# Decode attention on one core: K of a head, then V, softmax and PV in the same loop round, V as one 8 MB load

## The chip, the cores and the metric

One core of a Trainium2 chip. The metric is the device time of one execution in microseconds (us). A core has a tensor engine (PE), a vector engine (DVE), a scalar engine (ACT), a general engine (POOL), a sync engine (SP), which here only issues loads, and 16 DMA engines. The kernel before takes 422.17 us (median of 3 runs, 422.05 to 422.44).

## The reference

```python
h = layernorm(x) * (1 + ca) + sa            # x: 2 x 1 x 1024; sa, ca, ... = silu(c) @ w_mod
q = h @ wq                                  # 2 x 32 heads x 128
k, v = k_cache, v_cache                     # 2 x 4 kv heads x 32768 x 128, bf16; 8 q heads share one
p = softmax(q @ k.T * 128 ** -0.5)
x = x + ga * ((p @ v) @ wo)
h = layernorm(x) * (1 + cb) + sb
x = x + gb * (gelu(layernorm(h) @ w1 + b1) @ w2 + b2)
```

There is one new token and a cache of 134 MB. With the weights 178 MB are read; the arithmetic on them is small. "A head" below means one of the 8 pairs of batch and kv head: 8.4 MB of K and 8.4 MB of V.

## The kernel before

A load puts tokens on the 128 partitions. PE transposes K in groups of 8 tiles of 128x128 into PSUM (`tr`), DVE or ACT copies the group to SBUF, and PE multiplies it by the 8 query vectors (`qk`). When all 32 groups of a head are through, the softmax needs the maximum of each query (three small steps over DVE and PE), 8 exps on ACT, and then PE multiplies the probabilities by V (`pv`).

The kernel before hides the softmax: a loop round does K of head i together with softmax and PV of head i-1 ("lagged").

```python
for i in range(NBG):                         # 8 heads; folded into a hardware loop on PE and DVE
    lagged(softmax_1)                        # lagged(): of head i - 1, skipped in the first round
    for cc in range(NCH):                    # 4 chunks of K
        for g8 in range(TPC // 8):           # 8 groups of 8 tiles
            tr(i, cc, g8)
            ...
            if len(pipe) > PIPE: qk(*pipe.pop(0))
            if (cc, g8) == (0, 1):   lagged(softmax_2)
            elif (cc, g8) == (0, 4): lagged(softmax_3)
            elif i and (0, 4) < (cc, g8) and exps: exp(i - 1, exps.pop(0))
        if cc == 1:   lagged(lambda: pv(i - 1, 0), row_sums, lambda: pv(i - 1, 1))
        elif cc == 3: lagged(lambda: pv(i - 1, 2), lambda: pv(i - 1, 3))
    lagged(extract)
    while pipe: qk(*pipe.pop(0))
    lagged(lambda: extract_2(i - 1))
# after the loop: softmax, exps, PV of the last head, then wo, w1, w2
```

Loads are halves of a head (4 MB, 32 KB on each partition), each kind and half with its own 32 KB slot of a ring. SP issues them in program order, each when its slot is free:

```python
SLOT = {("K", 0): 0, ("V", 0): 1, ("K", 1): 2, ("V", 1): 3}
def add_kv(kind, i, hf):
    ...
    add((kind, i, hf), [2, TPC * D], cache[b, g][r0:r0 + 2 * CH_ROWS, :].rearrange("(p c t) d -> p c (t d)", c=2, p=128),
        SLOT[kind, hf] * 32 * KB, f"{kind}{hf}")
# order in the steady state: K half 0 of i, V half 0 of i-1, K half 1 of i, V half 1 of i-1
```

## Time and profile before

| | before |
|---|---|
| median time | 422.17 us |
| span in the profile | 420.3 us |
| DMA, mean over the span | 425 GB/s |
| PE busy | 296.6 us (71%) |
| chain that ended last | 70% DMA |

The page's row of slices cuts the span into 40 pieces. A digit is the busy share in tenths (9 is 90% or more), PEclk is PE's granted clock in tenths of full speed.

```profile
PE   1547429869988767695969686976859693645566
...
PEclk9999999988999997988888896989887888655575
DMA  8999999999999999999999999999999999999995
GB/s 335 430 430 420 437 440 443 411 437 446 409 443 443 424 430 443 433 421 443 440 418 443 437 418 440 443 415 440 449 412 440 446 416 437 423 429 423 428 426 244
```

The DMA row has no hole from the second slice to the last but one. The table of stretches for two heads in the middle says the same, with busy times (the number of instructions in brackets), PE's clock, DMA share and rate:

```profile
core 0: us, PE busy (x) PEld busy (x) DVE busy (x) ACT busy (x) POOL busy (x), PEclk, DMA share, GB/s
179.30:218.00 38.70, 30.43 (x585) 26.71 (x585) 19.18 (x36) 18.36 (x32) 0.31 (x2) 0.86 1.00 433
218.00:256.70 38.70, 30.80 (x584) 27.06 (x584) 19.23 (x36) 18.36 (x32) 0.31 (x2) 0.85 1.00 433
```

No compute engine is full. The groups of instructions (busy us and mean ns of one, then the idle time of the engine just before them and what ended most of it) show who waits:

```profile
L543 PE MATMUL psKT<-ident,K 128*128 128x128 bf16 x2048 | 174.0, 237 | 46.1 <-DMA K<-in_A_k_cache_dram 45.1
...
L576 ACT ACTIVATE E_sb<-S_sb,negm 128x256 bf16<-128x256 f32 x64 | 32.3, 504 | 8.1 <-DVE negm L572 7.1
L586 PE MATMUL psO<-V,E_sb 128*32 128x512 bf16 x512 | 33.9, 401 | 1.3 <-ACT E_sb L576 1.3
```

PE stood for 45 us waiting for K to land. The last head is not lagged, so its timeline (start, duration, engine, line; the idle time before and its releaser in brackets) shows beforehand what a serial round looks like:

```profile
353.67 0.17 DVE L572 TENSOR_SCALAR negm<-psM 128x8 f32<-128x8 f32 x1 [0.48 <-PE psM L571]
353.93 0.51 ACT L576 ACTIVATE E_sb<-S_sb,negm 128x256 bf16<-128x256 f32 x1 [3.60 <-DVE negm L572]
...
358.99 0.23 DVE L593 COPY rsum<-rowsum 128x128 f32<-128x128 f32 x1 [5.16 <-ACT E_sb L576]
359.27 0.59 PE L594 MATMUL psM<-onesf,rsum 128*128 128x1 f32 x2 [5.65 <-DVE rsum L593]
359.79 5.83 PE L586 MATMUL psO<-V,E_sb 128*32 128x512 bf16 x64
```

PE is idle 5.65 us while ACT does 8 exps, and PV's 64 matmuls then take 5.83 us. In the loop 16 of them take 1.05 us at full clock, 4.2 us for 64.

The chain of work that ended last, by engine and by line:

```profile
DMA 70%; PE 26%; ACT 2%; SPq 1%; issue 0%; DVE 0%
DMA K<-in_A_k_cache_dram 51%; PE psKT L543 18%; DMA wo<-in_A_wo_dram 8%; DMA w<-in_B_w_dram 7%; PE psS L555 5%; DMA wmod<-in_w_mod_dram 4%; ACT E_sb L576 1%; PE psO L586 1%; SPq L415 1%; ACT KT_sb L547 1%; PE psO L759 1%; PE psS L680 0%; ACT L576 0%; PE psM L566 0%; ACT S_sb L559 0%
```

### The profile page before, as it was taken

The numbers are of one execution on the slowest core, as the hardware profiler recorded it, in microseconds if no ns is written. First come the engines' busy times: TensorE is split into PE (matmuls) and PEld (weight loads), VectorE is DVE, ScalarE is ACT, GpSimd is POOL, SyncE is SP. The second block draws the span as 40 slices with busy tenths as digits, with TensorE's granted clock in tenths as the row PEclk, the third lists the DMA queues.
The fourth block names the chain that finished last, engine by engine and source line by source line (L and its number), as shares of the span: only waits on it lengthen the run. The fifth ranks groups of instructions, "written<-read, shape, count | busy, mean of one in ns | idle before, by whom it ended". The sixth has DMA issues, their size and how long they took to land.

```text
span 420.3 us, 11591 instructions
## 1 busy us (share of the span) xinstructions
PE 296.6 (71%) x5171; PEld 237.6 (57%) x5171; DVE 166.9 (40%) x347; ACT 156.2 (37%) x269; POOL 6.0 (1%) x31
## 2 busy tenths in 40 slices
PE   1547429869988767695969686976859693645566
PEld 1105109859878657494949575764849492212244
DVE  1102005645676454354536452653555363101311
ACT  2000005538548334551636282446426364200020
POOL 3000000000000000000000000000000000000000
PEclk9999999988999997988888896989887888655575
DMA  8999999999999999999999999999999999999995
GB/s 335 430 430 420 437 440 443 411 437 446 409 443 443 424 430 443 433 421 443 440 418 443 437 418 440 443 415 440 449 412 440 446 416 437 423 429 423 428 426 244
DMA packets 9727, 178.46 MB, mean 425 GB/s; under 512 B 1002, under 2 KB 1009, under 8 KB 2291
## 3 DMA queue, kind: packets, MB, share of 16 engines
q1 hardware_dynamic: 9714, 178.28, 98.9%
q8 instruction: 9, 0.15, 0.1%
q14 instruction: 4, 0.02, 0.0%
HBM read 178.28 MB, written 0.00 MB: 424 GB/s over the span
## 4 chain that ended last, share of the span: by engine, by line
DMA 70%; PE 26%; ACT 2%; SPq 1%; issue 0%; DVE 0%
DMA K<-in_A_k_cache_dram 51%; PE psKT L543 18%; DMA wo<-in_A_wo_dram 8%; DMA w<-in_B_w_dram 7%; PE psS L555 5%; DMA wmod<-in_w_mod_dram 4%; ACT E_sb L576 1%; PE psO L586 1%; SPq L415 1%; ACT KT_sb L547 1%; PE psO L759 1%; PE psS L680 0%; ACT L576 0%; PE psM L566 0%; ACT S_sb L559 0%
## 5 line engine op out<-in xcount | busy, mean ns | idle before, releaser
L543 PE MATMUL psKT<-ident,K 128*128 128x128 bf16 x2048 | 174.0, 237 | 46.1 <-DMA K<-in_A_k_cache_dram 45.1
L543 PEld LDWEIGHTS psKT<-ident,K 128*128 128x128 bf16 x2048 | 133.7, 106 | 53.7 <-DMA K<-in_A_k_cache_dram 49.2
L549 DVE COPY KT_sb<-psKT 128x1024 bf16<-128x1024 bf16 x160 | 107.8, 689 | 107.0 <-PE psKT L543 107.0
L547 ACT ACTIVATE KT_sb<-psKT 128x1024 bf16<-128x1024 bf16 x96 | 98.0, 1021 | 128.4 <-PE psKT L543 128.4
L555 PE MATMUL psS<-qcur,KT_sb 128*128 128x8 bf16 x2048 | 88.1, 167 | 7.7 <-ACT KT_sb L547 6.4
L555 PEld LDWEIGHTS psS<-qcur,KT_sb 128*128 128x128 bf16 x2048 | 79.0, 98 | 12.7 <-ACT KT_sb L547 7.6
L576 ACT ACTIVATE E_sb<-S_sb,negm 128x256 bf16<-128x256 f32 x64 | 32.3, 504 | 8.1 <-DVE negm L572 7.1
L586 PE MATMUL psO<-V,E_sb 128*32 128x512 bf16 x512 | 33.9, 401 | 1.3 <-ACT E_sb L576 1.3
L560 DVE TENSOR_REDUCE m1c<-psS 128x8 f32<-128x512 f32 x32 | 22.1, 690 | 14.8 <-ACT S_sb L559 14.1
L559 ACT ACTIVATE S_sb<-psS 128x512 f32<-128x512 f32 x32 | 18.9, 592 | 18.9 <-PE psS L555 18.9
L586 PEld LDWEIGHTS psO<-V,E_sb 128*32 128x32 bf16 x512 | 12.2, 100 | 13.1 <-issue 4.2
L491 PE MATMUL psS<-wmod,inT 128*32 128x512 bf16 x64 | 8.4, 622 | 11.9 <-DMA wmod<-in_w_mod_dram 11.9
L680 PE MATMUL psS<-wo,atT 128*32 128x512 bf16 x64 | 7.6, 627 | 10.8 <-DMA wo<-in_A_wo_dram 10.8
L462 ACT ACTIVATE stat<-stat 128x2 f32<-128x2 f32 x3 | 0.6, 203 | 35.4 <-DVE stat L461 35.4
L512 PE MATMUL psS<-wq,inT 128*32 128x512 bf16 x64 | 7.6, 627 | 7.1 <-DMA wq<-in_A_wq_dram 6.1
L576 ACT ACTIVATION_READ_ACCUMULATOR E_sb<-S_sb,negm 128x1 f32 x64 | 12.1, 189 | 0.0
L491 PEld LDWEIGHTS psS<-wmod,inT 128*32 128x32 bf16 x64 | 1.3, 112 | 17.9 <-DMA wmod<-in_w_mod_dram 17.4
L680 PEld LDWEIGHTS psS<-wo,atT 128*32 128x32 bf16 x64 | 1.9, 128 | 15.4 <-DMA wo<-in_A_wo_dram 9.4
L606 PE MATMUL psM<-msum,hmat 128*128 128x128 f32 x16 | 4.2, 346 | 7.1 <-DVE msum L601 7.1
L497 ACT ACTIVATE S_sb<-psS 128x512 f32<-128x512 f32 x1 | 0.6, 597 | 22.8 <-DVE S_sb L499 22.8
L499 DVE COPY S_sb<-psS 128x512 f32<-128x512 f32 x1 | 0.7, 692 | 20.6 <-PE psS L491 20.6
L599 DVE TENSOR_SCALAR msum<-psO,mk 128x128 f32<-128x128 f32 x8 | 2.8, 351 | 15.0 <-PE psO L586 15.0
(116 smaller groups left out, 136.4 us busy)
## 6 DMA issues: line engine op xcount, KB each, us to landing
K<-in_A_k_cache_dram SPq DMA_DIRECT2D x16, 4096.0 KB, 25.6
V<-in_A_v_cache_dram SPq DMA_DIRECT2D x16, 4096.0 KB, 32.5
wmod<-in_w_mod_dram SPq DMA_DIRECT2D x8, 1536.0 KB, 16.4
wq<-in_A_wq_dram SPq DMA_DIRECT2D x4, 2048.0 KB, 37.7
wo<-in_A_wo_dram SPq DMA_DIRECT2D x4, 2048.0 KB, 25.3
w<-in_B_w_dram SPq DMA_DIRECT2D x4, 1792.0 KB, 35.8
w<-in_B_w_dram SPq DMA_DIRECT2D x3, 2048.0 KB, 30.4
w<-in_B_w_dram SPq DMA_DIRECT2D x1, 768.0 KB, 27.9
```

The lines of the kernel that those rows point to most:

```text
L415: T.dma("sp", lambda e, dst=dst, src=cur.src: e.dma_start(dst, src), key=cur.sem, writes=[cur.reg], frees=old)
L491: pe(lambda e, w=it.view, k=k, ch=ch, n=n, q=q: e.matmul(bank[n][32 * q:32 * q + 32, :], lhsT=inT[:, k, :], rhs=w[:, ch * 512:(ch + 1) * 512],
L512: pe(lambda e, w=it.view, k=k, ch=ch, n=n, q=q: e.matmul(bank[n][32 * q:32 * q + 32, :], lhsT=inT[:, k, :], rhs=w[:, k % 2, ch * 512:(ch + ...
L543: pe(lambda e, kq=kq, jj=jj, w=kt, t=t: e.transpose(psKT[kq][:, jj * 128:(jj + 1) * 128], w[:, t, :], ident[:, :]), reads=[it.reg, "ident" ...
L547: act(lambda e, src=src: e.activation(KT_sb[g8][:, :, :], src, ACT.Copy), reads=[f"psKT{kq}"], writes=[f"KT_sb{g8}"], sem=f"ev{cc}_{g8}")
L549: dve(lambda e, src=src: e.tensor_copy(KT_sb[g8][:, :, :], src), reads=[f"psKT{kq}"], writes=[f"KT_sb{g8}"], sem=f"ev{cc}_{g8}")
L555: pe(lambda e, t=t, jj=jj: e.matmul(ps[:, t * HPG:(t + 1) * HPG], lhsT=KT_sb[g8][:, jj, :], rhs=qcur[:, :], start=True, stop=True), reads= ...
L559: act(lambda e: e.activation(Sc, ps[:, :].rearrange("p (t h) -> p h t", h=HPG), ACT.Copy), reads=[preg], writes=[f"S_sb{i % 2}_{cc}"], sem ...
L560: dve(lambda e: e.tensor_reduce(m1c[:, :, cc], ps[:, :].rearrange("p (t h) -> p h t", h=HPG), AX.X, ALU.max), reads=[preg], writes=[f"m1c{ ...
L576: act(lambda e: e.activation(E_sb[:, :, h, :], S_sb[j][:, h, :].rearrange("p (u t) -> p u t", t=4), ACT.Exp, bias=negm[:, h:h + 1], scale= ...
L586: pe(lambda e, t4=t4, tg=tg, q=q: e.matmul(psO[32 * q:32 * q + 32, :], lhsT=E_sb[:, tg // 4, :, :].rearrange("p h t -> p (h t)"), rhs=vt[: ...
L680: pe(lambda e, w=it.view, g=g, j=j, hf=hf, q=q: e.matmul(psS[0][32 * q:32 * q + 32, :], lhsT=atT[g][:, j, :], rhs=w[:, j, hf * 512:(hf + 1 ...
```

## The change

Its intent is a simpler loop: K of a head, then its softmax, then its V, all in one round; no second score buffer, no lag. V is wanted only at the end of a round, so it can be one load of 8 MB with 64 KB in a row for each partition, one slot, half as many packets. K stays in two loads. To make a partition's rows of V contiguous, the tokens are dealt to the partitions in another order, for K and V alike.

```diff
-    SLOT = {("K", 0): 0, ("V", 0): 1, ("K", 1): 2, ("V", 1): 3}
-    def add_kv(kind, i, hf):
-        ...
-        add((kind, i, hf), [2, TPC * D], cache[b, g][r0:r0 + 2 * CH_ROWS, :].rearrange("(p c t) d -> p c (t d)", c=2, p=128),
-            SLOT[kind, hf] * 32 * KB, f"{kind}{hf}")
+    def add_k(i, hf):
+        add(("K", i, hf), [2, TPC * D], A_k_cache[i % 2, i // 2].rearrange("(p h c t) d -> h p c (t d)", h=2, c=2, p=128)[hf], hf * 32 * KB, f"K{hf}")
+    def add_v(i):
+        add(("V", i), [NCH, TPC * D], A_v_cache[i % 2, i // 2].rearrange("(p c t) d -> p c (t d)", c=NCH, p=128), 64 * KB, "V")
...
+    for i in range(NBG):
+        add_k(i, 0)
+        add_k(i, 1)
+        add_v(i)
...
     for i in range(NBG):
-        lagged(softmax_1)
         for cc in range(NCH):
             for g8 in range(TPC // 8):
                 tr(i, cc, g8)
                 ...
-                if (cc, g8) == (0, 1): lagged(softmax_2)
-                ...
-            if cc == 1: lagged(lambda: pv(i - 1, 0), row_sums, lambda: pv(i - 1, 1))
-            elif cc == 3: lagged(lambda: pv(i - 1, 2), lambda: pv(i - 1, 3))
-        lagged(extract)
         while pipe:
             qk(*pipe.pop(0))
-        lagged(lambda: extract_2(i - 1))
+        softmax_1()
+        softmax_2()
+        softmax_3()
+        for h in range(HPG):
+            exp(h)
+        row_sums()
+        for cc in range(NCH):
+            pv(i, cc)
+        extract()
+        extract_2(i)
```

(The rest of the diff takes the machinery of the lag out of the helper that places waits, and the last head's copy out of the tail. The order of the loads becomes K, K, V of each head, and the slots of the w1 loads after the loop are dealt anew.)

More of the change, by code (lines that the diff above doesn't have):

```diff
@@ L34 @@
 RING = 160 * 1024
+AHEAD = ("sc2", "sc3", "pk", "ac")
 EVAC_PATTERN = ("dve", "act", "dve", "act", "dve", "dve", "act", "dve")
@@ L41 @@
     LOOPED = ("pe", "dve")
-    PE_KEYS = ("pe", "pl")
     def __init__(self, nc):
@@ L55, in __init__ @@
         self.segments = None
-        self.lag = False
     def key(self, name, given=0, step=None):
@@ L116, in _dep_tokens @@
         if E == "pe":
-            tokens = [t for t in tokens if t[0] not in self.PE_KEYS]
+            tokens = [t for t in tokens if t[0] != "pe"]
         return tokens
@@ L130, in _put @@
         if self.segments is not None and E in self.LOOPED:
-            self.segments[E][-1][1].append(op)
+            self.segments[E].append(op)
         else:
@@ L168, in raw @@
         self._put(E, ("raw", [], fn, None))
-    def part(self, lag):
-        self.lag = lag
-        for E in self.LOOPED:
-            self.segments[E].append((lag, []))
     def fold(self, rounds):
@@ L180, in _fold @@
         first = min(rounds)
-        full = rounds[max(rounds)]
         body = []
-        for n, (lag, ops) in enumerate(full):
-            merged = []
-            for k, (kind, _, fn, extra) in enumerate(ops):
-                offs = {}
-                for it, segs in rounds.items():
-                    same, other = segs[n]
-                    assert same == lag
-                    if not other and lag and it == first:
-                        continue
-                    assert len(other) == len(ops) and other[k][0] == kind and other[k][3] == extra
-                    for key, val in other[k][1]:
-                        off = val - self.step[key] * it
-                        assert offs.setdefault(key, off) == off, (E, n, k, key, it, val, offs)
-                waits = []
-                for key, off in offs.items():
-                    assert self.step[key] * (first + lag) + off > 0, (E, n, k, key, off)
-                    waits.append((key, self.step[key], off))
-                merged.append((kind, waits, fn, extra))
-            if merged:
-                body.append((lag, merged))
+        for k, (kind, _, fn, extra) in enumerate(rounds[max(rounds)]):
+            offs = {}
+            for it, ops in rounds.items():
+                assert len(ops) == len(rounds[first]) and ops[k][0] == kind and ops[k][3] == extra
+                for key, val in ops[k][1]:
+                    off = val - self.step[key] * it
+                    assert offs.setdefault(key, off) == off, (E, k, key, it, val, offs)
+            for key, off in offs.items():
+                assert self.step[key] * first + off > 0, (E, k, key, off)
+            body.append((kind, [(key, self.step[key], off) for key, off in offs.items()], fn, extra))
         self.ops[E].append(("loop", [], body, (first, max(rounds) + 1)))
@@ L218, in _loop @@
     def _loop(self, eng, E, body, bounds):
-        pairs = [w[1:] for _, ops in body for op in ops for w in op[1]]
+        pairs = [w[1:] for op in body for w in op[1]]
         often = [p for p in dict.fromkeys(pairs) if p != (1, 0) and pairs.count(p) > 1]
@@ L227, in wait @@
                 eng.wait_ge(self.sem[w[0]], val[w[1:]] if w[1:] in val else it * w[1] + w[2])
-            for lag, ops in body:
-                def run():
-                    for op in ops:
-                        self._emit(eng, E, op, wait)
-                if lag:
-                    with eng.If(it > bounds[0]):
-                        run()
-                else:
-                    run()
+            for op in body:
+                self._emit(eng, E, op, wait)
     def emit(self, block):
@@ L272, in bass_adaLN_cond__gqa_block_cached__mixer_channel_mlp__decode_kernel @@
     T = Tracker(nc)
-    for name, step, given in (("pe", 64, 0), ("pl", 8, 8), ("dve", 4, 0), ("dl", 4, 4)):
-        T.key(name, given)
-        T.step[name] = step
+    T.step["pe"], T.step["dve"] = 72, 8
     def sb(name, shape, dtype=FP32):
@@ L331, in bass_adaLN_cond__gqa_block_cached__mixer_channel_mlp__decode_kernel @@
     rinv = sb("rinv", [128, 1])
-    S_sb = [sb(f"S_sb{i}", [128, HPG, NT]) for i in range(2)]
-    row = S_sb[0].rearrange("p h n -> p (h n)")
-    ROW = [f"S_sb0_{cc}" for cc in range(NCH)]
+    S_sb = sb("S_sb", [128, HPG, NT])
+    row = S_sb.rearrange("p h n -> p (h n)")
+    ROW = [f"S_sb_{cc}" for cc in range(NCH)]
     E_sb = sb("E_sb", [128, NT // 4, HPG, 4], BF16)
@@ L368, in add @@
         by_key[key] = it
-    SLOT = {("K", 0): 0, ("V", 0): 1, ("K", 1): 2, ("V", 1): 3}
-    def add_kv(kind, i, hf):
-        cache = A_k_cache if kind == "K" else A_v_cache
-        b, g = i % 2, i // 2
-        r0 = hf * 2 * CH_ROWS
-        add((kind, i, hf), [2, TPC * D], cache[b, g][r0:r0 + 2 * CH_ROWS, :].rearrange("(p c t) d -> p c (t d)", c=2, p=128),
-            SLOT[kind, hf] * 32 * KB, f"{kind}{hf}")
+    def add_k(i, hf):
+        add(("K", i, hf), [2, TPC * D], A_k_cache[i % 2, i // 2].rearrange("(p h c t) d -> h p c (t d)", h=2, c=2, p=128)[hf], hf * 32 * KB, f"K{hf}")
+    def add_v(i):
+        add(("V", i), [NCH, TPC * D], A_v_cache[i % 2, i // 2].rearrange("(p c t) d -> p c (t d)", c=NCH, p=128), 64 * KB, "V")
     wm_v = w_mod.rearrange("(p k) n -> p k n", k=KT8)
@@ L383, in bass_adaLN_cond__gqa_block_cached__mixer_channel_mlp__decode_kernel @@
         add(("wq", k), [2, HQ * D], A_wq[k * 256:(k + 1) * 256, :].rearrange("(k p) n -> p k n", p=128), (96 + 16 * k) * KB)
-    add_kv("K", 0, 0)
-    add_kv("K", 0, 1)
-    order = [("K", 0), ("V", 0), ("K", 1), ("V", 1)]
-    early = [("V", 0), ("K", 0), ("K", 1), ("V", 1)]
-    for i in range(1, NBG + 1):
-        for kind, hf in early if i == 1 else order:
-            if kind == "V":
-                add_kv("V", i - 1, hf)
-            elif i < NBG:
-                add_kv("K", i, hf)
+    for i in range(NBG):
+        add_k(i, 0)
+        add_k(i, 1)
+        add_v(i)
     for g, off in enumerate((128, 144, 0, 16)):
         add(("wo", g), [8, DM], A_wo[g * 1024:(g + 1) * 1024, :].rearrange("(p j) n -> p j n", j=8), off * KB)
-    for k, off in enumerate((64, 80, 32, 48)):
+    for k, off in enumerate((32, 48, 64, 80)):
         add(("w1", k), [2, F], B_w1[k * 256:(k + 1) * 256, :].rearrange("(k p) n -> p k n", p=128), off * KB)
@@ L420, in dve @@
     def dve(fn, reads=(), writes=(), sem=None):
-        T.inst("dve", fn, reads=reads, writes=writes, sem=sem or ("dl" if T.lag else None))
+        T.inst("dve", fn, reads=reads, writes=writes, sem=sem)
     def act(fn, reads=(), writes=(), sem=None):
@@ L426, in pe @@
     def pe(fn, reads=(), writes=(), mark=True):
-        T.inst("pe", fn, reads=reads, writes=writes, mark=mark, sem="pl" if T.lag else None)
+        T.inst("pe", fn, reads=reads, writes=writes, mark=mark)
     need("wmod", 0)
@@ L522, in bass_adaLN_cond__gqa_block_cached__mixer_channel_mlp__decode_kernel @@
     dve(lambda e: e.tensor_copy(qT[:, :, :], psM[:, 0:64].rearrange("p (b h) -> p b h", b=2)), reads=["psM"], writes=["qT"], sem="mo")
-    for name in ("sc2", "sc3", "pk", "ac"):
-        T.key(name, 1)
-        T.raw("pe", lambda e, name=name: e.sem_inc(T.sem[name], 1))
-    for name in ("pl", "dl"):
-        T.raw("pe", lambda e, name=name: e.sem_inc(T.sem[name], T.step[name]))
+    for name in AHEAD:
+        T.key(name, T.step.get(name, 1))
+        T.raw("pe", lambda e, name=name: e.sem_inc(T.sem[name], T.step.get(name, 1)))
     T.wait("pe", reads=["ident", "identf", "onesf", "hmat"], writes=["psS0", "psS1", "psO", "psM"] + [f"psKT{q}" for q in range(NPKT)])
@@ L557, in qk @@
         if g8 == TPC // 8 - 1:
-            Sc = S_sb[i % 2][:, :, cc * TPC:(cc + 1) * TPC]
-            act(lambda e: e.activation(Sc, ps[:, :].rearrange("p (t h) -> p h t", h=HPG), ACT.Copy), reads=[preg], writes=[f"S_sb{i % 2}_{cc}"], sem=f"sc{cc}")
+            Sc = S_sb[:, :, cc * TPC:(cc + 1) * TPC]
+            act(lambda e: e.activation(Sc, ps[:, :].rearrange("p (t h) -> p h t", h=HPG), ACT.Copy), reads=[preg], writes=[f"S_sb_{cc}"], sem=f"sc{cc}")
             dve(lambda e: e.tensor_reduce(m1c[:, :, cc], ps[:, :].rearrange("p (t h) -> p h t", h=HPG), AX.X, ALU.max), reads=[preg], writes=[f"m1c{cc}"])
@@ L572, in softmax_3, with exp @@
         dve(lambda e: e.tensor_scalar(negm[:, :], psM[:, 128:128 + HPG], -SCALE, None, ALU.mult), reads=["psM"], writes=["negm"], sem="nm")
-    def exp(i, h):
-        j = i % 2
-        act(lambda e: e.activation(E_sb[:, :, h, :], S_sb[j][:, h, :].rearrange("p (u t) -> p u t", t=4), ACT.Exp, bias=negm[:, h:h + 1], scale=SCALE,
+    def exp(h):
+        act(lambda e: e.activation(E_sb[:, :, h, :], S_sb[:, h, :].rearrange("p (u t) -> p u t", t=4), ACT.Exp, bias=negm[:, h:h + 1], scale=SCALE,
                                    accum_out=rowsum[:, h:h + 1]),
-            reads=[f"S_sb{j}_{cc}" for cc in range(NCH)] + ["negm"], writes=["E_sb", "rowsum"], sem="ex" if h == HPG - 1 else None)
+            reads=ROW + ["negm"], writes=["E_sb", "rowsum"], sem="ex" if h == HPG - 1 else None)
     def pv(i, cc):
-        it = need("V", i, cc // 2)
-        vt = it.view[:, cc % 2, :]
+        it = need("V", i)
+        vt = it.view[:, cc, :]
         for t4 in range(TPC // 4):
@@ L620, in bass_adaLN_cond__gqa_block_cached__mixer_channel_mlp__decode_kernel @@
         T.segments = rounds[i + 1] = {E: [] for E in T.LOOPED}
-        def lagged(*fns):
-            T.part(True)
-            if i:
-                for fn in fns:
-                    fn()
-            T.part(False)
-        T.part(False)
-        exps = list(range(HPG))
-        lagged(softmax_1)
         for cc in range(NCH):
@@ L639, in bass_adaLN_cond__gqa_block_cached__mixer_channel_mlp__decode_kernel @@
                     qk(*pipe.pop(0))
-                if (cc, g8) == (0, 1):
-                    lagged(softmax_2)
-                elif (cc, g8) == (0, 4):
-                    lagged(softmax_3)
-                elif i and (0, 4) < (cc, g8) and exps:
-                    exp(i - 1, exps.pop(0))
-            if cc == 1:
-                lagged(lambda: pv(i - 1, 0), row_sums, lambda: pv(i - 1, 1))
-            elif cc == 3:
-                lagged(lambda: pv(i - 1, 2), lambda: pv(i - 1, 3))
-        lagged(extract)
         while pipe:
             qk(*pipe.pop(0))
-        lagged(lambda: extract_2(i - 1))
+        softmax_1()
[8 more added lines that the diff above has]
+        extract_2(i)
         T.segments = None
     T.fold(rounds)
-    T.lag = True
     for r0, r1 in ((0, 1), (1, 3), (3, 7), (7, 8)):
@@ L660, in bass_adaLN_cond__gqa_block_cached__mixer_channel_mlp__decode_kernel @@
     T.dma("sp", lambda e: e.dma_start(b1m[:, :], B_b1.rearrange("(q r) -> q r", r=512)), key="ld_b1", writes=["b1m"])
-    last = NBG - 1
-    softmax_1()
-    softmax_2()
-    softmax_3()
-    for h in range(HPG):
-        exp(last, h)
-    row_sums()
-    for cc in range(NCH):
-        pv(last, cc)
-    extract()
     for g in range(G):
         it = need("wo", g)
-        if g == 1:
-            extract_2(last)
         for j in range(8):
```

## The prediction

> **What bounds it now.** The DMA engines. The slice row shows them nine tenths busy or more nearly throughout; the stretch table of a head (179.3 to 218.0 us) has DMA share 1.00 at 433 GB/s, PE busy 30.4 of 38.7 us. The chain of waits is 70% DMA. The Trainium skill ("DMA: Bandwidth & Descriptors", Where 436 GB/s comes from) puts the fabric's ceiling at 435 GB/s; this trace agrees. Almost nothing can be won.
>
> **DMA side.** In the trace's packet records a 16 KB packet takes 611 ns, a 32 KB one 1213 ns: 9 ns fixed plus 36.7 ns per KB. Estimate for 64 KB: 2417 ns against 2 x 1213. Eight packets fewer per engine and head save 0.07 us a head, 0.6 us in all. A head takes about 38.8 us either way.
>
> **Compute side.** Softmax and PV of a head no longer hide under the next head's K; a PE round becomes serial. From the timeline:
> - K: 32 groups of transposes and QK at 0.645 us (full clock), and the last eviction: 21.2 us.
> - score copy, maxima, 8 exps (5.05 us), row sums, PE idle: 9.4 us (read from the last head, unlagged already).
> - PV: 4.2 us at full clock. The 9.4 us lets the clock fall to 0.5, as after 5 to 6 us of idle time in this trace ("TensorE: Matmul & The Clock Gate", Part 1, says this of an idle window); the last head's PV took 5.8 us. I take 6.0.
> - extraction of PV before the next K: 2.2 us; now and then a cold start of K, 0.4.
>
> Sum 39.2 us (38.3 to 40.5) against the DMA's 38.8: nearly equal, so slack decides. The first head's K ends at 88.7 us; the second head's K starts at about 106.5, 4.7 us after landing. The lag then changes by (round - 38.8), +0.4 us a head: 7 us at head 8.
> - V's single slot: the next V is issued when PV ends, 36 us into a round, and wanted at 48.5 us: no DMA gap until the lag is about 11 us. K's slots are free 18 us early.
> - Tail: no slack. From the last wo landing (382.8) PE and DVE run to the end without real waits. Four wo products need 3.6 us at full clock; they are in time while the last PV ends by about 378, a lag of up to 7 us. Beyond it every us of lag is a us of time, so each us of round length is worth 7.
>
> **Prediction.** 422.4 us: minus 0.6 for packets, plus about 1 for lag in the tail; range 421.0 to 428.0. Chances: faster by over 2% 0.01, within 2% 0.91, slower by over 2% 0.08.
>
> **What would show it.** Right: DMA share still 1.00 at 433 GB/s through the loop; V packets near 2417 ns; PE idle about 9 us before PV in each head, released by the exps; K transposes waiting for K's DMA far less than 45 us; heads 38.8 us apart. If PE's round is the longer one, the chain of waits moves from "DMA K" to PE and ACT, heads lie 39 to 40 us apart and the wo products come late, in a cluster. Wrong: gaps in the DMA row, the queue empty while SP waits for PV, or V packets slower than two of 32 KB.
>
> **What would make it wrong.** (1) The clock: cold through all of PV and into K, a round is 41 us and the time about 434. (2) Waits at the round's end that I have not seen (loop branch, reductions), which count seven times. (3) HBM reading less well at 64 KB steps between partitions. (4) 64 KB packets faster than the line through the smaller ones.

## The result, and the profile after

| | before | after |
|---|---|---|
| median time | 422.12 us (4 runs, 422.05 to 422.44) | 421.65 us (4 runs, 421.61 to 421.68) |
| span in the profile | 420.3 us | 419.9 us |
| PE busy | 296.6 us | 285.4 us |
| DMA packets | 9727 | 8573 |
| chain that ended last | 70% DMA, 26% PE | 50% PE, 30% DMA |

The ratio is 0.9987, 95% interval 0.997 to 1.0005: the same within 2%. (A ratio is the mean time of one kernel's fast runs over that of the other's fast runs of the same rounds, so not quite the ratio of the medians.)

The slices and the stretches of two heads, after:

```profile
PE   1547429856892898489559928965894699264575
...
PEclk9999858965997799599879969985998699686566
DMA  8999999999999999999999999999999999999995
GB/s 338 431 431 422 440 435 487 395 408 448 440 431 425 431 443 425 437 437 450 415 418 465 431 409 437 465 415 416 475 425 400 450 462 418 397 432 419 427 428 241
```

```profile
core 0: us, PE busy (x) PEld busy (x) DVE busy (x) ACT busy (x) POOL busy (x), PEclk, DMA share, GB/s
182.70:220.40 37.70, 28.08 (x585) 24.21 (x584) 19.15 (x36) 18.72 (x32) 0.31 (x2) 0.86 1.00 432
220.40:258.10 37.70, 28.09 (x586) 24.26 (x586) 19.16 (x36) 18.72 (x32) 0.31 (x2) 0.86 1.01 436
```

The DMA row is as full as before. (GB/s swings more from slice to slice; the share of busy time and the sums of the stretches do not.) A head's work on DVE is the same to 0.1 us and on ACT to 0.4 us. The groups that answer to those of before:

```profile
L506 PE MATMUL psKT<-ident,K 128*128 128x128 bf16 x2048 | 154.4, 221 | 8.0 <-DMA K<-in_A_k_cache_dram 6.4
...
L548 PE MATMUL psO<-V,E_sb 128*32 128x512 bf16 x512 | 44.6, 526 | 0.0
L538 ACT ACTIVATE E_sb<-S_sb,negm 128x256 bf16<-128x256 f32 x64 | 32.5, 507 | 23.8 <-DVE negm L535 22.0
L556 PE MATMUL psM<-onesf,rsum 128*128 128x1 f32 x16 | 4.7, 362 | 45.4 <-DVE rsum L555 45.4
```

PE's waits have moved. Before, 45.1 us of waiting for K; now 6.4 us (the first head alone), and 45.4 us of waiting for the row sums, which come after the exps. The idle time of PE stayed and changed its reason. One round's timeline shows its parts (K of this head began at 182.69):

```profile
202.59 1.30 PE L518 MATMUL psS<-qcur,KT_sb 128*128 128x8 bf16 x32
...
207.43 0.51 ACT L538 ACTIVATE E_sb<-S_sb,negm 128x256 bf16<-128x256 f32 x1 [2.90 <-DVE negm L535]
...
212.77 0.58 PE L556 MATMUL psM<-onesf,rsum 128*128 128x1 f32 x2 [5.65 <-DVE rsum L555]
213.29 5.07 PE L548 MATMUL psO<-V,E_sb 128*32 128x512 bf16 x64
...
218.41 0.35 DVE L561 TENSOR_SCALAR msum<-psO,mk 128x128 f32<-128x128 f32 x1 [4.84 <-PE psO L548]
...
219.97 0.49 PE L568 MATMUL psM<-msum,hmat 128*128 128x128 f32 x2 [1.62 <-DVE msum L563]
220.43 1.74 PE L506 MATMUL psKT<-ident,K 128*128 128x128 bf16 x28
```

K takes from 182.69 to 203.89, the softmax to 213.29, PV to 218.36, its extraction to 220.43. The same reading of all rounds gives this, beside the prediction:

| part of PE's round | predicted | measured, second to seventh round |
|---|---|---|
| K | 21.2 us, and 0.4 for a cold start | 21.2 in each, no cold start |
| last QK to PV | 9.4 | 9.2 to 9.8 |
| PV | 6.0 | 5.0 to 6.4 |
| extraction to the next K | 2.2 | 2.1 |
| round | 39.2 | 38.2 on the mean (106.64 to 335.76 us, six rounds) |

Last, the chain that ended last: its shares, and the part of it near the end, in order of time (start, duration, what):

```profile
PE 50%; DMA 30%; ACT 11%; DVE 6%; issue 2%; SPq 1%; ACTq 0%
PE psKT L506 27%; PE psS L518 10%; DMA K<-in_A_k_cache_dram 10%; PE psO L548 9%; DMA wo<-in_A_wo_dram 9%; ACT E_sb L538 8%; DMA w<-in_B_w_dram 7%; DMA wmod<-in_w_mod_dram 4%; DVE msum L563 2%; ACT KT_sb L510 2%; DVE m1c L523 1%; ACT S_sb L522 1%; PE psM L556 1%; PE psM L534 1%; PE psM L568 1%
```

```profile
345.02 0.47 PE psKT L506 x8
345.48 0.20 PE psS L518 x8
345.68 0.16 SPq L380
...
345.89 36.24 DMA wo<-in_A_wo_dram
...
382.17 1.65 PE psS L616 x13
383.82 30.20 DMA w<-in_B_w_dram
```

This looks as if PE now set the time. Whether it does is the main question for the experiments. The piece in the chain is the fourth wo load; it and the third went into a K slot that PE released, so the chain goes from that load to PE. But the piece "36.24 us DMA wo" runs from the issue to the landing: most of it is time in a queue that was full. An earlier issue would have made the load wait longer in the queue and land at the same time. A later run shows just that (the one with 72 transposes and no dose, below): its first wo load was issued at 331.1 us instead of 335.6 and landed at 367.7 instead of 367.6.

### The profile page after: what moved, and what is told of

The parts are those of the page before. It is cut to its first block, busy times and chain, and to the rows that moved or that the text cites. A ratio compares the mean times of both kernels' runs of the same rounds, so it can differ in the third digit from the quotient of the medians.

```text
span 419.9 us, 11452 instructions
## 1 busy us (share of the span) xinstructions
PE 285.4 (68%) x5171; PEld 225.2 (54%) x5171; DVE 167.3 (40%) x347; ACT 159.3 (38%) x269; POOL 5.9 (1%) x31
## 2 busy tenths in 40 slices
DMA packets 8573, 178.44 MB, mean 425 GB/s; under 512 B 873, under 2 KB 880, under 8 KB 2162
## 4 chain that ended last, share of the span: by engine, by line
PE 50%; DMA 30%; ACT 11%; DVE 6%; issue 2%; SPq 1%; ACTq 0%
PE psKT L506 27%; PE psS L518 10%; DMA K<-in_A_k_cache_dram 10%; PE psO L548 9%; DMA wo<-in_A_wo_dram 9%; ACT E_sb L538 8%; DMA w<-in_B_w_dram 7%; DMA wmod<-in_w_mod_dram 4%; DVE msum L563 2%; ACT KT_sb L510 2%; DVE m1c L523 1%; ACT S_sb L522 1%; PE psM L556 1%; PE psM L534 1%; PE psM L568 1%
## 5 line engine op out<-in xcount | busy, mean ns | idle before, releaser
L506 PE MATMUL psKT<-ident,K 128*128 128x128 bf16 x2048 | 154.4, 221 | 8.0 <-DMA K<-in_A_k_cache_dram 6.4
L506 PEld LDWEIGHTS psKT<-ident,K 128*128 128x128 bf16 x2048 | 118.7, 98 | 9.3 <-DMA K<-in_A_k_cache_dram 6.5
L518 PEld LDWEIGHTS psS<-qcur,KT_sb 128*128 128x128 bf16 x2048 | 76.9, 96 | 1.8 <-ACT KT_sb L510 1.4
L548 PE MATMUL psO<-V,E_sb 128*32 128x512 bf16 x512 | 44.6, 526 | 0.0
L556 PE MATMUL psM<-onesf,rsum 128*128 128x1 f32 x16 | 4.7, 362 | 45.4 <-DVE rsum L555 45.4
L548 PEld LDWEIGHTS psO<-V,E_sb 128*32 128x32 bf16 x512 | 16.9, 127 | 23.9 <-issue 19.5
L556 PEld LDWEIGHTS psM<-onesf,rsum 128*128 128x128 f32 x16 | 4.0, 310 | 46.1 <-DVE rsum L555 46.1
L555 DVE COPY rsum<-rowsum 128x128 f32<-128x128 f32 x8 | 1.8, 226 | 41.5 <-ACT E_sb L538 41.5
L529 PE MATMUL psM<-identf,m 128*8 128x128 f32 x16 | 3.4, 296 | 13.1 <-DVE m L526 13.1
L568 PEld LDWEIGHTS psM<-msum,hmat 128*128 128x128 f32 x16 | 2.4, 188 | 16.9 <-DVE msum L563 16.9
```

The source lines that it names most:

```text
L506: pe(lambda e, kq=kq, jj=jj, w=kt, t=t: e.transpose(psKT[kq][:, jj * 128:(jj + 1) * 128], w[:, t, :], ident[:, :]), reads=[it.reg, "ident" ...
L518: pe(lambda e, t=t, jj=jj: e.matmul(ps[:, t * HPG:(t + 1) * HPG], lhsT=KT_sb[g8][:, jj, :], rhs=qcur[:, :], start=True, stop=True), reads= ...
L548: pe(lambda e, t4=t4, tg=tg, q=q: e.matmul(psO[32 * q:32 * q + 32, :], lhsT=E_sb[:, tg // 4, :, :].rearrange("p h t -> p (h t)"), rhs=vt[: ...
L556: pe(lambda e: e.matmul(psM[:, 144:145], lhsT=rsum16.rearrange("p h e -> p (h e)"), rhs=onesf[:, 0:1], start=True, stop=True), reads=["one ...
L568: pe(lambda e: e.matmul(psM[:, 256:384], lhsT=hmat.rearrange("p h e -> p (h e)"), rhs=msum[:, :], start=True, stop=True), reads=["hmat", " ...
```

## The experiments

Theory: the DMA engines set the time of both kernels; the change costs nothing because PE's serial round (38.2 us) fits under the loads of a head (38.7) and the tail has slack; the half us won is the fixed cost of the packets that are gone. Rivals: PE's serial round is on the critical path, as the chain reads; the gain comes from the new order or the shorter program; what matters is only whether the DMA queue runs empty.

Twelve kernels were run. One thing makes ratios coarse here: in these rounds the kernel before had, besides its runs at 422.1 to 422.5 us, some at 423 to 425 that are classed fast as well (3 of 11 in the first set). I therefore name medians and lowest times. The change itself was not run again in these rounds; the kernel before was, and its lowest times (422.05 to 422.14 in all rounds) tie the sets together.

### One part undone: V in two loads of 32 KB per packet

```diff
-        add(("V", i), [NCH, TPC * D], ...rearrange("(p c t) d -> p c (t d)", c=NCH, p=128), 64 * KB, "V")
+        for hf in range(2):
+            add(("V", i, hf), [2, TPC * D], ...rearrange("(p h c t) d -> h p c (t d)", h=2, c=2, p=128)[hf], (64 + 32 * hf) * KB, f"V{hf}")
```

> The changed kernel with V of a head as two 4 MB loads of 32 KB per packet (its slots 32 KB each) instead of one 8 MB load of 64 KB; all else, the serial softmax and PV too, as in the change. Theory (the 0.5 us won are the fixed 9 ns of each packet): per engine and head 8 packets and one completion more, 9 x 9 ns x 8 heads = 0.65 us: 422.2 to 422.4. Rival (the 0.5 us come from the order of loads or from the shorter loop): 421.6 to 421.8. Rival (the late, single slot of V costs something that the packets hide): below 421.6.

Measured: 422.19 us (6 runs, 422.14 to 422.25), beside 422.25 for the kernel before (lowest 422.07). The 0.54 us of gain are gone, with the new order and the serial loop still in place. So the new order and the serial softmax by themselves cost and win nothing to within 0.1 us, and the gain is the packets'. 64 packets and 8 completions fewer per engine make 0.54 us: 7.5 ns each. The packet records, added up, give a better figure (one trace of each kernel): by 360 us this run has moved less than the change by 0.48 us of loading at 434 GB/s, but 0.14 us of that is there at 60 us, before any V is read. The loop adds 0.34 us, 4.7 ns for each of the 72.

### V in packets of 8 KB

```diff
-RING = 160 * 1024
+RING = 162 * 1024   # wo, w2 slots from 128 KB on moved up by 2 KB
-        add(("V", i), [NCH, TPC * D], ...)
+        add(("V", i), [8, 33 * D], ...rearrange("(p a x) d -> p a (x d)", p=128, a=8), 64 * KB, "V")   # 32 of each 33 rows loaded
```

> The changed kernel with V of a head as one 8 MB load of 8 KB per packet (units spread in SBUF with 256 B between them so that they cannot be merged; two KB more ring). Theory of a fixed cost per packet: 56 packets more per engine and head at 9 ns = 0.5 us a head, 4.0 us in all: 425 to 426.5, V packets of 309 ns as for the weights. Rival (packet size is of no account, the 0.5 us come from elsewhere): 421.6 to 422.

Measured: 424.0 us (6 runs, 423.85 to 424.1): 2.35 us above the change, where 4.0 was expected. The direction is right, the size not: 2.35 us over 448 packets are 5.2 ns each; by the bytes moved, counted in the same way, the loop loses 2.07 us, 4.6 ns each. The packet records of the trace give these durations (median):

```
 8 KB  309 ns      16 KB  611 ns      32 KB 1213 ns      64 KB 2418 ns
```

By these records eight packets of 8 KB take 54 ns more than one of 64 KB, which would be 3.5 us here; the execution lost less. The length of a record is not what a packet costs a full queue: about half of the 9 ns fitted to the records shows up in the time.

### PE's round made longer, in steps

To find the slack, transposes are repeated in the middle of each head's K, where PE is at full clock. They write what is written there anyway.

```diff
         kq = g8 % NPKT
+        if (cc, g8) == (1, 0):
+            for jj in range(8 * n):                # n = 2: 0.9 us, n = 4: 1.8 us, n = 8: 3.6 us
+                pe(lambda e, kq=kq, jj=jj, w=kt: e.transpose(psKT[kq][:, (jj % 8) * 128:(jj % 8 + 1) * 128], w[:, jj % 8, :], ident[:, :]),
+                   reads=[it.reg, "ident"], writes=[f"psKT{kq}"], mark=False)
```

In the changed kernel, n = 2:

> The changed kernel with 16 transposes repeated in the middle of each head's K: PE's round 0.9 us longer (about 39.1 us for 38.2), same results. Theory (DMA sets the time; a lag of PE is free until the last PV ends at about 378.5 us, now 371.7): 8 x 0.9 = 7.3 us of lag, just about the slack: plus 0 to 1.5 us, 421.7 to 423.2. Rival A (PE is on the critical path, as the chain of waits with 50% PE reads at its word): plus 7.3 us, 429. Rival B (a lag of PE only counts when the DMA queue runs empty): plus 0.

Measured: 427.68 us median, 424.14 to 427.87 (5 runs). The run of 424.14, the fastest of the five, is the one in the profile. It costs more than expected, though the rival of a PE that is critical at once (429) was not reached either.

In the changed kernel, n = 4:

> As before with 32 repeated transposes: PE's round 1.8 us longer, about 40.0 us, longer than the DMA's 38.8. Theory: 14.6 us of lag against 6.8 us of slack in the tail: plus 7 to 9 us, 428.5 to 430.5, with the DMA queue still full through V of the last head. Rival A (PE critical at once): plus 14.6 us, 436. Rival B (only an empty DMA queue counts): plus 0 to 2 us.

Measured: 434.91 us median, 432.41 to 437.7 (4 runs). The expectation of 428.5 to 430.5 missed, and the rival's 436 lies inside the spread. The traces show why. The timeline of the last head in this run, PE only, and PV's group:

```profile
386.98 0.59 PE L560 MATMUL psM<-onesf,rsum 128*128 128x1 f32 x2 [5.64 <-DVE rsum L559]
387.50 6.24 PE L552 MATMUL psO<-V,E_sb 128*32 128x512 bf16 x64
395.36 0.49 PE L572 MATMUL psM<-msum,hmat 128*128 128x128 f32 x2 [1.62 <-DVE msum L567]
395.78 3.64 PE L620 MATMUL psS<-wo,atT 128*32 128x512 bf16 x64
```

```profile
L552 PE MATMUL psO<-V,E_sb 128*32 128x512 bf16 x512 | 48.8, 565 | 0.0
```

Three things are to be seen. The 64 wo products come at once after the last PV (3.64 us without a wait), as predicted for a PE that is late. PV takes 6.1 to 6.25 us from the second head on, where the changed kernel had 5.5 on the mean of its second to seventh round. And a round is 40.8 us (109.86 to 354.89, six rounds), 2.65 us longer for a dose of 1.8. The dose was right (K went from 21.2 to 23.0); the rest is mainly PV at the lower clock. The times fit the slack rule of the prediction: PV of the last head may end at about 378.5 us, and what is later is lost.

| run | last PV ends | past 378.5 | span against the change (419.9) |
|---|---|---|---|
| change | 371.7 | none | |
| 16 transposes | 381.2 | 2.7 | +2.5 |
| 32 transposes | 393.7 | 15.2 | +13.9 |

This fit does not show that the time is lost in the tail. V has one slot, so a late PV also issues the next V late. With 32 transposes the DMA queue ran empty, or all but, before V of the fourth head and of each later one (five gaps of 1.3 to 1.7 us in the packet records, where a full queue was expected; at the first gap PE's fourth head began 10.6 us after its K had landed). Added up from the packet records, its loads were 12.9 us behind those of the change at 360 us, before the last PV. With 16 transposes the queue did not run empty, but from 180 us on V's packets took 2.44 us on the mean (2.42 in the change) and single ones 3.5, and the loads were 1.6 us behind at 360 us. And PE's last large step waits for a w2 load in the change (first line) as with 32 transposes (second line):

```profile
414.06 2.88 PE L695 MATMUL psO<-gT,w 128*128 128x2 bf16 x96 [1.08 <-DMA w<-in_B_w_dram]
428.04 2.83 PE L699 MATMUL psO<-gT,w 128*128 128x2 bf16 x96 [0.47 <-DMA w<-in_B_w_dram]
```

That load landed at 414.0 us in the change, at 416.6 with 16 transposes and at 428.0 with 32: 2.6 and 14.0 us later, which is the whole cost to 0.1 us. PE's own chain after the last PV was only 0.5 us shorter with 32 transposes, so the two limits nearly coincide, and these runs do not separate a PE that is late in the tail from a queue that a late PE has starved. That PE's round is the cause of both is what the next section shows.

### The clock, tested by itself

PE gets work while ACT does the exps: 72 transposes of the identity into a buffer that is free. Nothing is taken away; each round has 72 matmuls more.

```diff
         softmax_3()
+        for jj in range(72):
+            pe(lambda e, jj=jj: e.transpose(psKT[0][:, (jj % 8) * 128:(jj % 8 + 1) * 128], ident[:, :], ident[:, :]),
+               reads=["ident"], writes=["psKT0"], mark=False)
         for h in range(HPG):
             exp(h)
```

On top of the 32 transposes that cost 13 us:

> The run with 32 repeated transposes (434.9 us), and in addition 72 transposes of the identity, issued by PE before it waits for the row sums, so that PE has work while ACT does the exps (same results). Theory (the excess over the dose comes from PV at the half clock, 6.2 us instead of 4.2): PV 4.2 us in every head, rounds about 39 us, last PV at about 378: 421.7 to 424. Rival (the excess has another cause; more PE work only lengthens the round): 434 or more.

Measured: 421.83 us (4 runs, 421.8 to 421.94), against 434.91 without them: more work, 13 us less. PV's group and the chain's shares:

```profile
L552 PE MATMUL psO<-V,E_sb 128*32 128x512 bf16 x512 | 29.1, 380 | 0.0
```

PV is 3.64 us a head in place of 6.2, the last PV ends at 372.4, and the time is back at the DMA's. So the excess over the dose was PE's clock after its idle time. The Trainium skill ("TensorE: Matmul & The Clock Gate", Part 1) says that the array runs at half rate after an idle window of about 3.4 us until a busy one has passed. The clock records of the change change state only in steps of 3.41 us, in the middle of the loop 27.31 us at full and 10.24 us (once 13.65) at half clock in turn. With the dose it is 27.31 and 13.65, with the 72 transposes on top 34.13 and 3.41. In these rounds the clock rises from half to full while PE does nothing but the 72 transposes (134.8 to 140.6 us in the second head, the rise at 138.9).

The same 72 transposes in the changed kernel without a dose are the direct test of "PE 50%":

> The changed kernel with only the 72 transposes of the identity while ACT does the exps (no dose, same results): PV at the full clock, PE's round about 36.3 us instead of 38.2 until it waits for K's loads. Theory (DMA sets the time of the changed kernel, although its chain of waits reads 50% PE): 421.5 to 421.9, nothing won, and K's transposes wait for the loads again, by more than 10 us in sum. Rival (PE's serial round is on the critical path): 1.9 us a head less, down to 408.

Measured: 421.82 us (6 runs, 421.73 to 421.98). PE's round is up to about 2 us shorter (142.81 to 178.96 us, 36.2, for the third head) and nothing is won. PE waits for K's loads again; its waits (total us, times, longest), and the chain:

```profile
PE psKT L506 <- DMA K<-in_A_k_cache_dram: 11.6, 4, 6.4
```

```profile
DMA 50%; PE 41%; DVE 3%; ACT 3%; issue 2%; SPq 1%; ACTq 0%
```

PE found K not yet landed in the fourth, sixth and eighth head (at 179.13, 256.45 and 333.86 us), which also times the loads: 38.7 us a head. (Of the 11.6 us, 6.4 are the first head's, as in the change; 5.2 are new.) The rival, under which the time would have fallen towards 408, is out. (The time is 0.17 us above the change's. By the packet records 0.12 us of it are there at 60 us, before the first of these transposes runs at 93.4.)

### The same dose in the kernel before

n = 8 in the kernel before, twice the larger dose above:

> The kernel before with 64 transposes repeated in the middle of each head's K (3.6 us a head, twice what made the changed kernel 13 us slower). Theory: with softmax and PV lagged PE waits over 5 us a head for K's loads, so the dose disappears there: 422.0 to 423.0. Rival (extra work on PE costs the same in both kernels, what hurt the changed kernel is not its serial round): plus 13 us or more.

Measured: 425.81 us median (4 runs, 425.66 to 426.51), 3.5 us more than the 422.33 of before; 422 to 423 was expected, 13 us more or beyond by the rival. The table of stretches finds the loss in one place:

```profile
core 0: us, PE busy (x) PEld busy (x) DVE busy (x) ACT busy (x) POOL busy (x), PEclk, DMA share, GB/s
...
90.00:100.00 10.00, 9.18 (x200) 8.52 (x201) 6.05 (x12) 5.52 (x8) 0.19 (x1) 1.00 0.74 288
...
110.00:150.00 40.00, 37.37 (x804) 32.84 (x797) 22.41 (x43) 21.64 (x37) 0.31 (x2) 1.00 1.00 433
```

There the second half of the second head's K was issued at 92.8 us, when the queue had just run out; in the kernel before it was issued at 87.0. From 110 us on the DMA share is 1.00 again in spite of 3.6 us more work in every head. By the packet records it is a single gap, of 2.7 us, with slower packets beside it: the loads are 3.9 us behind the kernel before at 100 us and still 3.9 at 340. Half the dose:

> The kernel before with 32 repeated transposes a head, the same 1.8 us a head that made the changed kernel 13 us slower. The run with 64 cost 3.5 us, all of it in one DMA gap at 90 to 100 us, because the second half of the second head's K was issued at 92.8 us when the queue ran out at 92. Theory: with half the dose it is issued at about 90 us, in time, and PE's waits for K swallow the rest: 422.0 to 423.0. Rival (the cost of a dose is in proportion, there is no threshold): plus 1.7 us, 423.9.

Measured: 424.25 us (4 runs, 424.04 to 424.58), against 422.75 for before on this chip (422.14 to 425.05). My expectation missed, and the rival's number, 423.9, is nearer. Still the loss is not spread over the heads: the packet records show one gap again, of 1.3 us, at the same place, with the load issued at 90.6 us, and the loads 1.7 us behind at 100 us as at 340. So the spot is thinner than I took it for, as a load needs some time between its issue and its first packet (in the run with 64, issued at 92.8, the packets began again at 93.8). It remains that the lagged kernel pays once at its second head, and the serial kernel with the same dose pays 13 us.

### Half of V

If both kernels stand on the DMA's time but one has no room beneath it, fewer bytes must tell them apart. V's slots are half filled and used twice (wrong results).

```diff
 before:  -  [2, TPC * D] ... "(p c t) d -> p c (t d)"            +  [1, TPC * D] ... [:, 0:1, :]      pv reads view[:, 0, :]
 change:  -  [NCH, TPC * D] ... "(p c t) d -> p c (t d)"          +  [2, TPC * D] ... [:, 0:2, :]      pv reads view[:, cc % 2, :]
```

> The kernel before, with half of V loaded and each loaded half used twice (wrong result on purpose): a head's loads take 29.1 us instead of 38.8. Theory: here PE's round without waits is 29 to 31 us, so about 8 us a head are won: 350 to 362 us. Rival (the two kernels have the same bound at every load size): the same gain as in the changed kernel.

> The changed kernel, with the first half of V loaded and used twice (wrong result on purpose): a head's loads take 29.1 us. Theory: PE's serial round of 38 us stays, so nothing is won in the loop; only the tail starts at once after the last PV (371.7) instead of waiting for wo to land: minus 5 to 8 us, 413 to 417. Rival (DMA alone sets the time): 350 to 362 as for the kernel before.

Measured: the kernel before, 362.74 and 365.87 us (the other two runs, 370.3 and 370.4, and the profile lie over 1.5% above the fastest; their granted clock of 0.90 was not lower, so it may be this kernel's own spread. With them the gain would be 52 us at least). The changed kernel, 411.53 us median, 408.75 to 412.74. The same bytes saved bring the kernel before about 58 us and the changed kernel about 11. Both missed my ranges by a few us: the former gained less than expected, the latter more. In the changed kernel's trace the loop is as it was (K of the last head starts at 336.2 us, 335.8 in the change) and all of the gain comes after the last PV. So the serial round is a second bound, 38.2 us a head, just beneath the first.

### An attempt to do better

If a packet costs 5 to 7.5 ns wherever it is, w_mod's loads can be joined in the same way.

```diff
-    for k in range(KT8):
-        add(("wmod", k), [6 * DM], wm_v[:, k, :], k * 12 * KB)
+    for k in range(KT8 // 2):                      # or KT8 // 4, 48 KB
+        add(("wmod", k), [2, 6 * DM], wm_v[:, 2 * k:2 * (k + 1), :], k * 24 * KB)
```

> The changed kernel with w_mod in four loads of 24 KB per packet instead of eight of 12 KB: 32 packets an engine fewer. Theory (a packet costs 5 to 7.5 ns of a full queue's time, as the runs with 32 KB and 8 KB packets of V showed, wherever it is): minus 0.15 to 0.3 us, 421.3 to 421.5, the fastest of all. Rival (only V's packets matter, or it is lost in the wait for the first larger load): 421.6 or more.

> As before with two loads of 48 KB per packet: 48 packets an engine fewer. Theory of the packets: minus 0.25 to 0.4 us, 421.2 to 421.4, provided that the later start of PE on w_mod (half of it lands at once, then the other half) stays hidden behind the queue of wq and K. Rival (PE's later start delays wq, q or K's slots): 422 or more.

Measured: 422.05 us (6 runs, 421.74 to 422.82) and 422.06 (421.93 to 422.51), beside 422.75 (422.14 to 425.05) for the kernel before. The lowest times are 0.40 and 0.21 us under that of before; the change itself was 0.47 under its before by medians and 0.44 by lowest times. So there is no gain over the change to be seen. From the start of the first large packet to the end of the last one it was 414.5 us in the change, 414.5 with 24 KB and 414.8 with 48 KB. By the bytes moved (one trace each) the packets do save as expected: between 5 and 60 us the two runs gain 0.16 and 0.23 us on the change, 5 ns a packet. But at 5 us they are 0.17 and 0.23 us behind it. Eight other traces, with w_mod as in the change (the kernel before among them), are 0.11 to 0.15 us behind it there too, so it is the change's trace that started early, and why is not known. No version was found that is clearly faster than the change.

## Why the prediction was right

- **The bound.** Right: the DMA row stays full, the loop runs at 432 to 436 GB/s, and a PE round made about 2 us shorter won nothing. The Trainium skill ("DMA: Bandwidth & Descriptors", Where 436 GB/s comes from) puts the fabric's ceiling at 435 GB/s, and both traces run within 1% of it.
- **Packets, minus 0.6 us.** Right in kind, shown by the run with 32 KB packets; measured 0.47 (medians) and 0.54. The 64 KB packet took 2418 ns, 2417 predicted (its slope of 36.7 ns is per 1000 bytes). But the 9 ns a packet were too much: 4.6 to 4.7 ns by the bytes moved in the loop, which is 0.34 us of the 0.6; what is won beyond that lies before the first V.
- **PE's round, 39.2 us.** Measured 38.2. K, softmax and extraction were right to 0.2 us on the mean. The terms too large were PV (6.0; 5.5 on the mean) and the cold start of K (0.4; none). The estimate of 4.2 us for PV at full clock, four times a short PV of the kernel before, was too large as well: 3.64 us when it ran at full clock.
- **"Plus about 1 for lag in the tail."** This step was not borne out: with a round of 38.2 the lag does not grow by 0.4 us a head, it shrinks by about 0.5. At the eighth head K had landed at about 333.9 us (from the run in which PE waited for it) and started at 335.8: 1.9 us of lag, 7 predicted. The last PV ended at 371.7, 6.8 us early. So the lag that was left cost nothing in the tail.
- **The slack of the tail, 378 us.** It fits two runs with a late PE, to 1.3 us, but is not shown by itself: in both runs the loads were behind before the tail, by 1.6 and 12.9 us. The other limit that the prediction named, no gap in the DMA until the lag is about 11 us, was met: the first gap came at a lag of 10.6.
- **"Each us of round length is worth 7."** Not shown as it stands. With 32 transposes most of the loss was in the queue, before the tail, and the clock had its part: a dose of work also moves PV against the clock's windows; 1.8 us of work became 2.65 us of round. The prediction had this as its first danger, a cold PV and a round of 41 us, "about 434": the run with 32 transposes, a round of 40.8 and 434.9 us, is that case.
- **The sign in the profile.** One of the signs was wrong: the prediction took a chain of waits that moves to PE as proof that PE's round is the longer one. The chain did move (26% to 50% PE) and PE's round was not longer. It passes through slots that PE releases long before the queue needs them.
- **Rivals.** "PE is critical" is out by the run that shortens PE's round. "The order or the program brings the gain" is out by the run with 32 KB packets. "Only an empty queue counts" is out in its strict form, plus 0: the 16 transposes cost 2.5 us in a profile in which the queue never ran empty. But 1.6 us of these, and 12.9 of the 13.9 us of the 32 transposes, were already lost in the loads before the last PV, so that the queue is one way, and perhaps the main one, in which a late PE costs time is not ruled out.

Open: the kernel before's second level of 423 to 425 us; the spread of the run with 16 transposes (424.1 and four at 426.8 to 427.9), which fits a PV that falls differently on the clock's windows, but only one of these runs has a trace; how much of a late PE's cost arises in the tail and how much in the queue; and why the change's own trace is 0.1 us ahead of the others at its start. 64 KB packets in the lagged kernel were not tried: with a lag the old V is still in use when the next must come, and two slots of 64 KB leave 32 KB of the ring's 160, room for half of K.

## What to carry to other kernels

Before software-pipelining a loop whose loads fill the DMA engines, add up the serial round from the timeline and compare it with the loads' time of one round: if it fits beneath, the lag buys no time, only room, and the room is what a later saving of bytes will need. Where the two are within a few per cent, the margin is to be measured by a dose of known work, because idle time has a price of its own in the tensor engine's clock and a little more work in the gap can make the kernel faster. A chain of waits that leads through a buffer's release says who released it, not that an earlier release would help: look first whether the queue was full. Where it is not full, a late release does cost: count the bytes moved by a given time in two traces and see where one falls behind.

## What the Trainium skill lacked or had wrong

- "DMA: Bandwidth & Descriptors", Specifications and Why small descriptors are slow: line rate from 512 B on, a fixed overhead of about 3 cycles for each packet, and packing descriptors called worth it only up to 256 B. In a full queue a packet's cost can be seen far above that: 8 KB packets of V in place of 64 KB cost 2.35 us in 424, 32 KB in place of 64 KB 0.54 us; by the bytes moved in the loop 4.6 and 4.7 ns a packet.
- "TensorE: Matmul & The Clock Gate", Part 1: the half clock after idle windows is as the runs show it. What is lacking is that a loop's length depends on how it lies to the windows: the half-clock stretches were 10.24 us long in the change and 13.65 us with 1.8 us more work, and the round grew by 2.65 us. Its section Why this matters for your kernels says to leave no idle gap over about 3 us, but not that idle matmuls can fill one, nor what that is worth: 13 us in the run with the dose, nothing where the DMA was the bound.
- No page that I read says that a chain of waits counts time in a full DMA queue as a transfer: 36.24 us for a wo load of 2 MB, in a kernel whose DMA moves 8.4 MB in 19.3 us (8 packets of 2418 ns on each engine).
